# Attention step: the order of its products on TensorE, and the dealing of its output products over the column groups

## The chip, the cores and the metric

The kernel runs on one core of one Trainium2 chip. The metric is the device time of one execution in microseconds (us), the median over the runs of a kernel. A core has a matrix engine (TensorE, PE in the profile, with its weight loads shown apart as PEld), VectorE (DVE), ScalarE (ACT), GpSimd (POOL) and SyncE (SP), which issues most of the DMAs. Each engine works through a list of instructions of its own, in the order in which the program wrote them.

## The reference

Eight batches of eight heads go through attention over 576 positions with windows, and the result goes through a mixture of eight experts, of which each token uses two.

```python
# attention: batch 8, heads 8, seq 576, head_dim 64
scores = q @ k.T / 8
rel = pos[:, None] - pos[None, :]
mask_plain = (rel >= 0) & (rel < 32)                         # heads 0 to 3
mask_dil = (rel >= 0) & (rel < 128) & (rel % 4 == 0)         # heads 4 to 7
attn = softmax(where(mask, scores, -1e9))
x = (attn @ v) as rows of 512 per token                      # 4608 tokens
# experts: D 512, E 8, F 1024
noisy = x @ w_gate + log1p(exp(x @ w_noise)) * noise
top2 = the two largest of noisy; weights = softmax over the two
out[token] = sum over the two: weight * (relu(x @ w1[e]) @ w2[e])
```

## The kernel before

The program has an attention stage and an expert stage. The change lies in the attention stage.

**Attention.** The work is cut into 24 steps. Two batches make a unit `u` (four units), a unit has two groups `g` (first the four heads with the dilated mask, then the four with the plain one), and a group has three steps `st`; step `k` is `3 * g + st`. With the layout chosen, a query block of 32 rows sees 64 keys, so the products are small. One step does this:

- `qk(k)`: the mask is put into the PSUM tile `s` by two products with an identity (L360, 128 columns of weights, bf16), then 24 products of queries and keys add the scores (L371). Each of them has 32 columns of weights, and its 32 output partitions say which of the four column groups of TensorE it uses. VectorE then takes the maximum of each row (L376) and subtracts it, writing `a` (L377). There is one buffer of `s`.
- `expo(k)`: ScalarE takes the exponential of `a` into `pe` (L382).
- `ptr(k)`: six transposes of `pe` through TensorE into the PSUM tiles `pp` (L396, 128 columns), which ScalarE copies to `pt` in two copies (L397).
- `pv(k)`: 24 output products of `pt` and the values into `o` (L414, 32 columns of weights, 130 moving columns, the last of a head being the sum of the row). VectorE computes the reciprocal of the sums (`den`, L421 and L423) and the scaled `x` (L426).
- `move_x(k)` and `store_x(k)`: ScalarE moves a part of `x` (L434), and SP writes it to DRAM (L439, L441).
- `x_transpose(k)`: six transposes of `x` into `xtp` (L449, 128 columns) and two copies to `xt` on ScalarE (L451).
- `gate_mm(k)`: eight products of `xt` with the gate's weights (L471, 32 columns) and copies to `gs` on ScalarE (L476, L497).
- `gate_front(u, st)`: three transposes of `gs` (L509, 128 columns) and one VectorE reduction (L510), three times for each unit when the unit is done.

A matmul of f32 operands appears in the trace as two records where its weights have 32 columns, so 24 products are 48 records.

The steps are staggered in a loop over `i`: an iteration runs `qk(i)`, `move_x(i - 2)`, `ptr(i - 1)`, `store_x(i - 2)`, `x_transpose(i - 2)`, `expo(i)`, `pv(i - 1)`, `gate_front` if one is due and `gate_mm(i - 2)`, in this order. Nothing reorders what the program writes: the order of calls is the order on each engine. Between the calls, `micro(n)` takes the next few small operations from the generators `gate(t0, n)`, which choose the experts for blocks of tokens (VectorE operations of 0.1 to 0.6 us, L524 to L628), and `fillers(kb)` runs what `at(kb, ...)` put on a slot; an iteration has the slots `2 * i` and `2 * i + 1`. The loads of the next keys, queries and values and of the first expert's weights hang on such slots.

**Experts.** After the loop the eight experts run one after another (`up`, L826, and `down_tile`, L868), with the gathers of their tokens (L770, L778), weights and scatters (L845) planned by a clock of TensorE columns. The first expert's tokens are gathered and split (L792, L797, L798, through the same PSUM tag `tin` as `xtp`) while the attention still runs.

Of the kernel before, what the change touches and what calls it, by code (L numbers as in the profile page):

```python
# [46 lines left out]
def attention_moe_kernel(ctx, tc, qt, kp, kd, vpl, vdl, w_gate, w_noise, noise, w1, w2, out, CAPS=(1216, 1216, 1216, 1184, 1184, 1152, 1152, 1152), SPLITS=(0, 384, 896)):  # L47
# [306 lines left out]
    def qk(k):  # L354
        g, st = divmod(k, 3)
        ty = 1 - g % 2
        s = aps.tile([128, 8, 2, 64], F32, name="s", tag="s")
        for e in (0, 4):
            n = min(4, 6 - e)
            tensor.matmul(s[:, e:e + n], lhsT=identb,  # L360
                          rhs=masks[ty][:, 6 * st + e:6 * st + e + n].unsqueeze(2).to_broadcast([128, n, 2, 64]),
                          start=True, stop=False, skip_group_check=True)
        for e in range(6):
            for qd in range(4):
                if ty == 0:
                    x = qd // 2
                    b, ub = divmod(12 * st + 6 * (qd % 2) + e, 18)
                else:
                    x = qd
                    b, ub = divmod(6 * st + e, 9)  # L370
                tensor.matmul(s[32 * qd:32 * qd + 32, e], lhsT=QV[ty][:, b, x, 32 * ub:32 * ub + 32],  # L371
                              rhs=KV[ty][:, :, b, x, 32 * ub:32 * ub + 64],
                              start=False, stop=True, skip_group_check=True)
# [26 lines left out]
    def pv(k):  # L400
# [4 lines left out]
        for hh in range(4):  # L405
            for r, a, jp, b, ub in blocks(st, ty):
# [517 lines left out]
    fronts = {6 * u + 6 + st: (u, st) for u in range(U) for st in range(3)}  # L924
# [39 lines left out]
    for t0, n, kb in ((0, 9, 17), (9, 9, 29), (18, 6, 39), (24, 3, 41), (27, 6, 51)):  # L964
        at(kb, lambda t0=t0, n=n: gens.append(gate(t0, n)))
    L0 = 12 * (U - 1)
    at(29, lambda: (new_idx(0), gens.append(idx_late(list(gens), 0, SPLITS[1], lambda: x_block(0)))))
    at(41, lambda: gens.append(idx_late(list(gens), SPLITS[1], SPLITS[2], lambda: x_block(1))))
# [39 lines left out]
    for i in range(NS + 2):  # L1008
# [3 lines left out]
        early[0] = False  # L1012
        if i < NS:
            qk(i)
# [4 lines left out]
        if 1 <= i <= NS:  # L1019
            ptr(i - 1)  # L1020
        micro(2)
        micro(2)
        fillers(2 * i)
        if i >= 2:
            store_x(i - 2)
            x_transpose(i - 2)
        if i < NS:

            expo(i)
        micro(2)  # L1030
        if 1 <= i <= NS:
            pv(i - 1)
        micro(2)
        if i >= 2:
            if i in fronts:
                gate_front(*fronts.pop(i))
            gate_mm(i - 2)
# [4 lines left out]
    for f in fronts.values():  # L1042
# [191 lines left out]
```

## Time and profile before

| what | value |
|---|---|
| median of three runs | 1081.24 us (1080.13 to 1085.15) |
| span of the profiled execution | 1086.8 us; no time beside the span is given for it |
| PE busy | 1011.7 us (93%) |
| PEld busy | 855.7 us (79%) |
| DVE, ACT, POOL busy | 465.7, 319.4, 534.5 us |
| first mask product of the first step | 9.6 us |
| first product of the first expert | 227.24 us |

The attention stage is the first fifth of the span; from 227.24 us on TensorE works on the experts. The span of the profiled execution is 5.6 us above the median of the runs. A row of the timeline reads: start in us, length in us, engine, line, operation, tile written and tiles read, shape, count of records and, in brackets, how long the engine had been idle before and what ended it. "issue" is time in which an engine waited for nothing that the profile shows.

### The profile page before, as it was taken

The page shows a single profiled execution, that of the slowest core. Times are in us where ns is not written, and L with a number is a line of the kernel's source. Part 1 is how long each engine was busy: PE and PEld are TensorE (multiplying, and loading weights), DVE is VectorE, ACT ScalarE, POOL GpSimd, SP SyncE. Part 2 cuts the span into 40 slices and gives each one's busy share as a digit, 9 for nine tenths or more (in the row PEclk, how much of TensorE's full clock was granted, in tenths as well). Part 3 has the DMA queues.
Part 4 walks back from the last instruction along what each step waited for, and adds up shares of the span by engine and source line. Part 5 has one row for each costly group of instructions (what it writes and reads, how often), then busy time and mean ns, then how long its engine had stood idle before and what let it go on. Part 6 is the DMA issues. An engine that isn't in the chain of part 4 may idle for free. (4 is left out here: it accounts for less than half of the span.)

```text
span 1086.8 us, 18768 instructions
## 1 busy us (share of the span) xinstructions
PE 1011.7 (93%) x7274; PEld 855.7 (79%) x7275; DVE 465.7 (43%) x1060; ACT 319.4 (29%) x609; POOL 534.5 (49%) x727
## 2 busy tenths in 40 slices
PE   6896877778989999999999999999999999999996
PEld 4774655567878989988997889788978888888885
DVE  7673635635225444344434352435353434343221
ACT  6673534622113322222223131312131222222110
POOL 7004243455776655755644564466455645553112
PEclk9998887878999999999999999999999999999999
DMA  8898687455255243533533352426242623453123
GB/s 280 313 315 278 194 283 257 151 164 186 43 96 129 54 109 85 109 84 86 91 85 85 86 131 50 102 64 135 38 112 52 137 39 108 75 119 72 24 28 45
DMA packets 79214, 132.95 MB, mean 122 GB/s; under 512 B 31648, under 2 KB 41296, under 8 KB 77840
## 3 DMA queue, kind: packets, MB, share of 16 engines
q1 hardware_dynamic: 56768, 92.56, 27.6%
q0 software_dynamic: 22352, 39.15, 19.6%
q8 instruction: 58, 0.95, 0.4%
q14 instruction: 36, 0.29, 0.1%
HBM read 92.11 MB, written 39.54 MB: 121 GB/s over the span
## 5 line engine op out<-in xcount | busy, mean ns | idle before, releaser
L826 PE MATMUL up<-x,w1h 128*128 128x512 f32 (+4 forms) x1536 | 396.7, 344 | 10.9 <-issue 8.2
L778 POOL DMA_INDIRECT g<-xs,ixi x258 | 269.7, 1045 | 84.0 <-issue 78.6
L826 PEld LDWEIGHTS up<-x,w1h 128*128 128x128 f32 x1536 | 273.1, 189 | 37.2 <-issue 8.7
L826 PE MATMUL up<-x,w1l 128*128 128x384 f32 (+4 forms) x768 | 263.4, 343 | 0.0
L868 PE MATMUL dn<-w2h,hh 128*128 128x512 f32 x576 | 225.5, 392 | 0.0
L868 PE MATMUL dn<-w2l,hh 128*128 128x512 f32 x576 | 224.7, 390 | 0.0
L868 PE MATMUL dn<-w2h,hl 128*128 128x512 f32 x576 | 224.6, 390 | 0.0
L832 DVE SCALAR_TENSOR_TENSOR hl<-up,hh 128x384 fp32r<-128x384 f32 (+2 forms) x192 | 106.7, 557 | 249.1 <-ACT hh L830 187.0
L830 ACT ACTIVATE hh<-up 128x384 fp32r<-128x384 f32 (+4 forms) x192 | 94.6, 498 | 298.7 <-PE up L826 248.7
L845 POOL DMA_INDIRECT out_rows<-y,ixs x67 | 107.3, 1602 | 141.4 <-DVE y L877 119.0
L826 PEld LDWEIGHTS up<-x,w1l 128*128 128x128 f32 x768 | 145.4, 189 | 11.8
L877 DVE TENSOR_SCALAR y<-dn,ixs 128x512 f32<-128x512 f32 x63 | 47.3, 751 | 188.2 <-PE dn L868 163.5
L868 PEld LDWEIGHTS dn<-w2h,hl 128*128 128x128 f32 x576 | 108.4, 188 | 22.7
L868 PEld LDWEIGHTS dn<-w2h,hh 128*128 128x128 f32 x576 | 108.5, 188 | 22.0
L868 PEld LDWEIGHTS dn<-w2l,hh 128*128 128x128 f32 x576 | 108.5, 188 | 21.8
L797 ACT CAST x<-xr 128x512 fp32r<-128x512 f32 x67 | 40.5, 605 | 216.0 <-DVE xr L795 175.8
L306 POOL COPY spacer<-hh 1x1 f32<-1x1 f32 x72 | 26.4, 366 | 131.9 <-ACT hh L830 131.6
L628 POOL DMA_INDIRECT tab<-en,si x72 | 71.8, 998 | 36.1 <-issue 16.2
L798 DVE TENSOR_TENSOR x<-xr,x 128x512 fp32r<-128x512 f32 x67 | 44.7, 667 | 17.9 <-ACT x L797 12.4
L371 PE MATMUL s<-kt,qt 128*32 128x128 f32 x1152 | 41.2, 288 | 9.9 <-DMA qt<-in_qt 5.4
L371 PEld LDWEIGHTS s<-kt,qt 128*32 128x32 f32 x1152 | 32.5, 115 | 20.3 <-issue 19.6
L708 DVE TENSOR_TENSOR w1l<-ws,w1h 128x1024 fp32r<-128x1024 f32 x32 | 38.8, 1218 | 20.8 <-ACT w1h L706 10.9
(186 smaller groups left out, 867.2 us busy)
## 6 DMA issues: line engine op xcount, KB each, us to landing
ws<-in_moe_w SPq DMA_DIRECT2D x36, 512.0 KB
ws<-in_moe_w SPq DMA_DIRECT2D x112, 128.0 KB
out_rows<-zero SPq DMA_DIRECT2D x38, 256.0 KB
vd<-in_vdl SPq DMA_DIRECT2D x24, 390.0 KB
vp<-in_vpl SPq DMA_DIRECT2D x16, 585.0 KB
qt<-in_qt SPq DMA_DIRECT2D x14, 576.0 KB
xs<-x SPq DMA_DIRECT2D x24, 256.0 KB
kt<-in_kd SPq DMA_DIRECT2D x16, 320.0 KB
```

The costliest lines, as they stand in the source:

```text
L371: tensor.matmul(s[32 * qd:32 * qd + 32, e], lhsT=QV[ty][:, b, x, 32 * ub:32 * ub + 32], rhs=KV[ty][:, :, b, x, 32 * ub:32 * ub + 64], star ...
L628: ins = gpsimd.indirect_dma_start(out=tab, out_offset=bass.IndirectOffsetOnAxis(ap=si[:, kq, t:t + 1], axis=0), in_=en[:, kq, t], in_offse ...
L708: return lambda: vector.tensor_tensor(b, s, a.bitcast(F32), op=OP.subtract)
L778: gpsimd.indirect_dma_start(out=g[:, j], out_offset=None, in_=xq, in_offset=bass.IndirectOffsetOnAxis(ap=IX[e][1][:, r0 // 32 + j:r0 // 32 ...
L797: scalar.copy(xh[:, :, o:o + rn], xr[:, :, 0:rn])
L798: return lambda: vector.tensor_tensor(xl[:, :, o:o + rn], xr[:, :, 0:rn], xh[:, :, o:o + rn].bitcast(F32), op=OP.subtract)
L826: tensor.matmul(p[:, 0:n], lhsT=a[:, 128 * f:128 * f + 128], rhs=b[:, kc, 0:n], start=(i == 0), stop=(i == 11))
L830: scalar.activation(hh[:, f, 0:n], p[:, 0:n], AF.Relu)
L832: vector.scalar_tensor_tensor(hl[:, f, 0:m], p[:, 0:m], 0.0, hh[:, f, 0:m].bitcast(F32), op0=OP.max, op1=OP.subtract)
L845: ins = gpsimd.indirect_dma_start(out=out, out_offset=bass.IndirectOffsetOnAxis(ap=sc[0:rn, t, 1:2], axis=0), in_=y[0:rn], in_offset=None, ...
L868: tensor.matmul(p[0:rn], lhsT=a[:, f, o:o + rn], rhs=b[:, f % 2], start=(i == 0), stop=(i == 23))
L877: vector.tensor_scalar(y[0:rn], p[0:rn], wsc, None, op0=OP.mult)
```

## The change

The mask products get a function of their own, `mask_scores(k)`, and the loop is written in another order: first what uses 128 columns of weights (`x_transpose`, `gate_front`, the mask, `ptr`), then what uses 32 (`qk`, `gate_mm`, `pv`). `x_transpose` and `gate_mm` now belong to step `i - 3`, one iteration later than before; the last three are caught up at the end. `gate_front` is one iteration later as well, and the slots on which the generators start are moved by one. `expo(i)` is written behind `pv(i - 1)`. In `pv`, the 16 products of rows 0 to 3 come first, in turn over the four column groups, and then the 8 of rows 4 and 5, for the heads in the order 0, 2, 1, 3.

```diff
+    def mask_scores(k):
+        s = SC[k] = aps.tile([128, 8, 2, 64], F32, name="s", tag="s")
+        for e in (0, 4):
+            n = min(4, 6 - e)
+            tensor.matmul(s[:, e:e + n], lhsT=identb,
...
     def qk(k):
-        s = aps.tile([128, 8, 2, 64], F32, name="s", tag="s")
-        for e in (0, 4):
-            n = min(4, 6 - e)
-            tensor.matmul(s[:, e:e + n], lhsT=identb,
...
+        s = SC.pop(k)
...
     def pv(k):
-        for hh in range(4):
-            for r, a, jp, b, ub in blocks(st, ty):
+        bl = list(blocks(st, ty))
+        for hh, rows in [(hh, bl[0:4]) for hh in range(4)] + [(hh, bl[4:6]) for hh in (0, 2, 1, 3)]:
+            for r, a, jp, b, ub in rows:
                 qd, c0 = (r, hh) if r < 4 else (2 * (r - 4) + hh // 2, 4 + hh % 2)
...
-    fronts = {6 * u + 6 + st: (u, st) for u in range(U) for st in range(3)}
+    fronts = {6 * u + 7 + st: [(u, st)] for u in range(U - 1) for st in range(3)}
+    fronts[6 * U + 1] = [(U - 1, 0), (U - 1, 1)]
+    fronts[6 * U + 2] = [(U - 1, 2)]
...
-    for t0, n, kb in ((0, 9, 17), (9, 9, 29), (18, 6, 39), (24, 3, 41), (27, 6, 51)):
+    for t0, n, kb in ((0, 9, 18), (9, 9, 30), (18, 6, 40), (24, 3, 42), (27, 6, 50)):
         at(kb, lambda t0=t0, n=n: gens.append(gate(t0, n)))
...
     for i in range(NS + 2):
         micro(2)
+        if 3 <= i < NS:
+            x_transpose(i - 3)
+        micro(2)
+        for f in fronts.pop(i, []):
+            gate_front(*f)
         if i < NS:
-            qk(i)
+            mask_scores(i)
+        micro(2)
+        if 1 <= i <= NS:
+            ptr(i - 1)
         micro(2)
         if i >= 2:
             move_x(i - 2)
         micro(2)
-        if 1 <= i <= NS:
-            ptr(i - 1)
-        micro(2)
-        micro(2)
         fillers(2 * i)
         if i >= 2:
             store_x(i - 2)
-            x_transpose(i - 2)
         if i < NS:
-            expo(i)
+            qk(i)
         micro(2)
+        if 3 <= i < NS:
+            gate_mm(i - 3)
         if 1 <= i <= NS:
             pv(i - 1)
-        micro(2)
-        if i >= 2:
-            if i in fronts:
-                gate_front(*fronts.pop(i))
-            gate_mm(i - 2)
+        if i < NS:
+            expo(i)
+        for k in {NS: (NS - 3, NS - 2), NS + 1: (NS - 1,)}.get(i, ()):
+            micro(2)
+            x_transpose(k)
+            gate_mm(k)
         micro(2)
         micro(2)
         fillers(2 * i + 1)
```

**TensorE, one step with a `gate_front`.** Lines in the changed program stand seven or eight further down: L362 is the mask, L378 `qk`, L403 `ptr`, L422 `pv`, L457 `x_transpose`, L479 `gate_mm`, L517 `gate_front`. Before:

```order
L360 MATMUL s<-mask_144,identb 128x512
L360 LDWEIGHTS identb
L360 MATMUL s<-mask_144,identb 128x256
L371 MATMUL s<-kt_98,qt_100 32x128 x24
L396 MATMUL pp_194<-ident,pe 128x128 x4
L396 MATMUL pp_195<-ident,pe 128x128 x2
L449 MATMUL xtp<-ident,x 128x128 x6
L414 MATMUL o<-vd,pt 32x130 x24
L509 MATMUL gt<-ident,gs 128x128 x3
L471 MATMUL pp_195<-xt,wg 32x128 x4
L471 MATMUL pp_195<-xt,wg 32x64 x4
```

The same engine in the changed program, from one `x_transpose` to the next:

```order
L457 MATMUL xtp<-ident,x 128x128 x6
L517 MATMUL gt<-ident,gs 128x128 x3
L362 LDWEIGHTS identb
L362 MATMUL s<-mask_144,identb 128x512
L362 LDWEIGHTS identb
L362 MATMUL s<-mask_144,identb 128x256
L403 MATMUL pp_194<-ident,pe 128x128 x4
L403 MATMUL pp_195<-ident,pe 128x128 x2
L378 MATMUL s<-kt_98,qt_100 32x128 x24
L479 MATMUL pp_195<-xt,wg 32x128 x4
L479 MATMUL pp_195<-xt,wg 32x64 x4
L422 MATMUL o<-vd,pt 32x130 x24
```

The change between 128 and 32 columns of weights came six times in such a step (four times without `gate_front`) and now comes twice; the transposes of `pe` (`ptr`) stood behind the next step's `qk` and now stand ahead of it.

**ScalarE, the same step.** Before, from the move of `x` to the copies of `gs`:

```order
L434 COPY x<-x 32x2x128 x2
L397 COPY pt<-pp_194 128x512
L397 COPY pt<-pp_195 128x256
L451 COPY xt<-xtp 128x384 x2
L382 ACTIVATE pe<-a 128x6x2x64
L476 COPY gs<-pp_195 64x6x32 x2
```

In the changed program:

```order
L459 COPY xt<-xtp 128x384 x2
L404 COPY pt<-pp_194 128x512
L404 COPY pt<-pp_195 128x256
L442 COPY x<-x 32x2x128 x2
L484 COPY gs<-pp_195 64x6x32 x2
L389 ACTIVATE pe<-a 128x6x2x64
```

The exponential moved from ahead of the copies of `gs` to behind them, and the copies of `xt` to the front.

**VectorE, the step in which the second `gate` runs**: the last rows ahead of the maximum of the next step's scores. Before:

```order
L549 MAX u_1897<-nl 128x8 x6
L423 RECIPROCAL den<-den 128x12
L553 MAX_INDEX c_1899<-u_1897,nl 128x8 x6
L426 TENSOR_TENSOR x<-o,den 128x384 x2
L553 MAX_INDEX c_1899<-u_1897,nl 128x8 x3
L557 TENSOR_TENSOR wd<-u_1897 128x9
L560 CAST xf<-c_1899 128x18
L564 TENSOR_TENSOR oh<-i_168,xf 128x72 x2
L567 TENSOR_TENSOR ob<-oh 128x72
L572 TENSOR_SCALAR ns<-xf 128x9
L574 TENSOR_SCALAR ns<-ns 128x2x9
L376 TENSOR_REDUCE mx<-s 128x12
```

In the changed program (L383 is the maximum, L434 the scaled `x`):

```order
L541 TENSOR_TENSOR c_1930<-c_1930,nl 128x72
L434 TENSOR_TENSOR x<-o,den 128x384 x2
L548 TENSOR_TENSOR l_1929<-l_1929,c_1930 128x72
L550 TENSOR_TENSOR l_1929<-l_1929,nz 128x72
L552 TENSOR_TENSOR nl<-l_1929,lg 128x72
L557 MAX u_1928<-nl 128x8 x9
L561 MAX_INDEX c_1930<-u_1928,nl 128x8 x9
L565 TENSOR_TENSOR wd<-u_1928 128x9
L568 CAST xf<-c_1930 128x18
L572 TENSOR_TENSOR oh<-i_168,xf 128x72 x2
L575 TENSOR_TENSOR ob<-oh 128x72
L383 TENSOR_REDUCE mx<-s 128x12
```

The operations of `gate` that stood between `den` and `x` now stand behind `x`, in one piece ahead of the next maximum.

More of the change, by code (lines that the diff above doesn't have):

```diff
@@ L352, in attention_moe_kernel @@
     SB, PE_, PT, XG, XT, GS = {}, {}, {}, {}, {}, {}
-    def qk(k):
+    SC = {}
+    def mask_scores(k):
         g, st = divmod(k, 3)
         ty = 1 - g % 2
-        s = aps.tile([128, 8, 2, 64], F32, name="s", tag="s")
+        s = SC[k] = aps.tile([128, 8, 2, 64], F32, name="s", tag="s")
         for e in (0, 4):
@@ L362, in qk @@
                           start=True, stop=False, skip_group_check=True)
+    def qk(k):
+        g, st = divmod(k, 3)
+        ty = 1 - g % 2
+        s = SC.pop(k)
         for e in range(6):
@@ L962, in x_block @@
             plan(US_X[bi - 1] + 3.0 * i, lambda t=t: split_first(bi, t))
-    for t0, n, kb in ((0, 9, 17), (9, 9, 29), (18, 6, 39), (24, 3, 41), (27, 6, 51)):
+    for t0, n, kb in ((0, 9, 18), (9, 9, 30), (18, 6, 40), (24, 3, 42), (27, 6, 50)):
         at(kb, lambda t0=t0, n=n: gens.append(gate(t0, n)))
     L0 = 12 * (U - 1)
-    at(29, lambda: (new_idx(0), gens.append(idx_late(list(gens), 0, SPLITS[1], lambda: x_block(0)))))
-    at(41, lambda: gens.append(idx_late(list(gens), SPLITS[1], SPLITS[2], lambda: x_block(1))))
+    at(30, lambda: (new_idx(0), gens.append(idx_late(list(gens), 0, SPLITS[1], lambda: x_block(0)))))
+    at(42, lambda: gens.append(idx_late(list(gens), SPLITS[1], SPLITS[2], lambda: x_block(1))))
     at(2, setup_a)
@@ L1025, in attention_moe_kernel @@
             store_x(i - 2)
-            x_transpose(i - 2)
+        if i < NS:
[3 more added lines that the diff above has]
+            gate_mm(i - 3)
+        if 1 <= i <= NS:
+            pv(i - 1)
         if i < NS:
             expo(i)
-        micro(2)
-        if 1 <= i <= NS:
-            pv(i - 1)
-        micro(2)
-        if i >= 2:
-            if i in fronts:
-                gate_front(*fronts.pop(i))
-            gate_mm(i - 2)
+        for k in {NS: (NS - 3, NS - 2), NS + 1: (NS - 1,)}.get(i, ()):
+            micro(2)
+            x_transpose(k)
+            gate_mm(k)
         micro(2)
@@ L1041, in attention_moe_kernel @@
     early[0] = True
-    for f in fronts.values():
+    for f in sum(fronts.values(), []):
         gate_front(*f)
```

## The prediction

> **What bounds the kernel now.** I read the page first, then the busy time by stage, the waits of the attention stage, and last the timeline of single steps, because an average over the stage hides which wait ends last. Here and below, 0.5% of the time, 5.4 us, is about what a measurement of this kernel can tell from no change.
>
> ```profile
> span 1086.8 us, 18768 instructions
> ...
> PE 1011.7 (93%) x7274; PEld 855.7 (79%) x7275; DVE 465.7 (43%) x1060; ACT 319.4 (29%) x609; POOL 534.5 (49%) x727
> ...
> PEclk9998887878999999999999999999999999999999
> ```
> ```profile
> 40.00:60.00 20.00, 20.00 (x462) 16.48 (x460) 12.85 (x31) 14.77 (x36) 0.43 (x1) 1.00 0.92 320
> 80.00:100.00 20.00, 13.59 (x189) 10.49 (x189) 7.32 (x25) 6.74 (x14) 8.77 (x16) 0.80 0.95 318
> 140.00:160.00 20.00, 15.09 (x213) 9.98 (x206) 6.11 (x21) 5.95 (x14) 11.53 (x22) 0.75 0.88 285
> 340.00:1087.00 747.00, 734.66 (x3660) 634.76 (x3658) 291.17 (x458) 174.59 (x291) 386.00 (x470) 1.00 0.40 84
> ```
>
> The columns behind the length of a stretch are PE, PEld, DVE, ACT and POOL, the granted clock, the DMAs' share and GB/s. From 340 us on PE is busy 735 of 747 us at full clock: the experts are bound by PE, so what the attention stage saves or loses arrives at the end. From 40 to 60 us PE is busy all the time. From 80 to 100 and from 140 to 160 it is not, the clock is 0.80 and 0.75, and the DMAs are at 0.95 and 0.88. So the attention stage is of two kinds. How much of each, the mask's rows tell (48 records in 24 steps):
>
> ```profile
> L360 PE MATMUL s<-mask,identb x48: 270/378/609, 9.6 to 197.8; 128*128 128x512 bf16 x24, 128*128 128x256 bf16 x24
> ```
> ```profile
> PEld s L371 <- issue: 19.6, 28, 4.4
> PE o L414 <- ACT pt L397: 11.9, 7, 4.3
> DVE mx L376 <- remote: 20.6, 3, 8.4
> ```
>
> Between the first and the last step lie 188 us for 23 steps, 8.2 us each. Nine of these 23 gaps are 5.37 to 6.01 us (five of them with a `gate_front`); the other 14 hold about 60 us more than that, in which engines wait for nothing that the profile shows ("issue") or for "remote", DVE once for 8.4 us.
>
> An undisturbed step without `gate_front`, and behind it the end of the next step, which has one:
>
> ```profile
> 41.90 0.50 PE L360 MATMUL s<-mask,identb 128*128 128x512 bf16 x2
> 42.33 1.52 PE L371 MATMUL s<-kt,qt 128*32 128x128 f32 x48
> 43.78 0.87 PE L396 MATMUL pp<-ident,pe 128*128 128x128 f32 x6
> 44.49 0.82 PE L449 MATMUL xtp<-ident,x 128*128 128x128 f32 x6
> 45.24 1.56 PE L414 MATMUL o<-vp,pt 128*32 128x130 f32 x44
> ...
> 47.28 0.50 PE L360 MATMUL s<-mask,identb 128*128 128x512 bf16 x2
> ...
> 50.63 1.78 PE L414 MATMUL o<-vp,pt 128*32 128x130 f32 x48
> 52.35 0.55 PE L509 MATMUL gt<-ident,gs 128*128 128x128 f32 x3
> 52.82 0.54 PE L471 MATMUL pp<-xt,wg 128*32 128x128 f32 x16
> 53.29 0.50 PE L360 MATMUL s<-mask,identb 128*128 128x512 bf16 x2
> ```
>
> From mask to mask these take 5.38 and 6.01 us, PE in one row without a wait.
>
> **The change, PE's work.** A `gate_front` adds 0.63 us. Its three transposes cost 3 x 0.118 (six take 0.71, from 43.78 to 44.49), so the two extra changes between 128 and 32 columns cost 0.27, 0.14 each. The change goes from four to two of them without `gate_front`, from six to two with it: 0.27 and 0.54 us saved. The dealing: 48 records of `qk`, in turn over the groups, take 1.45 us for 128 columns, so 130 columns in turn should take 1.47; the old order takes 1.72 (50.63 to 52.35): 0.25 saved. PE's work of a step becomes 4.86 and 5.22 us.
>
> [...]
>
> **The change, the loop that it closes.** Before, `ptr` of a step stood behind the next step's `qk` and had more than 2 us to spare. Now `ptr(i - 1)` stands ahead of `qk(i)`, and it needs the exponential of step i - 1, which needs the subtraction, the maximum and `qk(i - 1)`. So one step cannot be shorter than that chain. Its pieces:
>
> ```profile
> 39.62 0.38 ACT L397 COPY pt<-pp 128x256 f32<-128x256 f32 x1
> 108.52 0.96 DVE L377 TENSOR_TENSOR a<-s,mx 128x768 f32<-128x768 f32 x1
> 109.51 0.90 ACT L382 ACTIVATE pe<-a 128x768 f32<-128x768 f32 x1 [0.31 <-DVE a L377]
> 111.35 1.52 PE L371 MATMUL s<-kt,qt 128*32 128x128 f32 x48
> 112.94 0.96 DVE L376 TENSOR_REDUCE mx<-s 128x12 f32<-128x768 f32 x1 [1.03 <-PE s L371]
> 114.00 0.96 DVE L377 TENSOR_TENSOR a<-s,mx 128x768 f32<-128x768 f32 x1
> 124.08 0.86 ACT L397 COPY pt<-pp 128x512 f32<-128x512 f32 x2 [4.49 <-remote]
> 124.72 2.83 PE L414 MATMUL o<-vd,pt 128*32 128x130 f32 x44 [4.26 <-ACT pt L397]
> ```
>
> From the start of `qk` to the maximum 1.59, to the subtraction 1.06, to the exponential 0.99 (108.52 to 109.51), the exponential 0.90. From ScalarE to PE: the first copy of the pair ends 0.86 - 0.38 = 0.48 behind 124.08, at 124.56, and PE starts at 124.72: 0.16. Then six transposes and the change to 32 columns, 0.75 (as from 44.49 to 45.24). Sum 5.45. To that comes the first weight load, which can't be made ahead any more; no row has it alone, it lies between nothing and 0.15 (about the 0.14 of a change of columns). I take 5.5, with 5.45 and 5.6 as the ends. PE's own work, 4.86 or 5.22, fits under it, so PE now waits 0.3 to 0.6 us a step. The mask doesn't add to this: it needs the subtraction, about 2.1 us behind `qk`, and PE comes to it only after `gate_mm`, `pv` and `x_transpose`. ScalarE doesn't either: the copies of `gs` (five small ones, about 1.1 us), which now stand ahead of the exponential, follow a `gate_mm` that ends 0.5 us behind `qk`, so they are done 1.6 us behind it, and the subtraction at 2.1.
>
> [...]
>
> **The sum.**
> 1. The nine undisturbed gaps: four without `gate_front` +0.12 each, five with it -0.51 each: -2.1 us. With the loop at 5.45 it is -2.5, at 5.6 -1.2.
> 2. The disturbed ones. PE's clock falls after a long wait, and then PE's work is what counts: `pv` took 2.83 for 44 records at 124.72 and 1.56 at 45.24, 1.8 times. A step wholly at that clock has 9.7 us of PE work before and 8.75 after, against a loop of about 7.3 (1.8 us more in `qk` and `ptr`): -0.95, with `gate_front` -1.4. I count seven such stretches, each about three quarters of a step: -5. Bounds: 0 (the wait sets the end, not the work behind it) and -9 (14 x 0.52 to 0.79, at full clock).
> 3. VectorE in steps with `gate`. The loop leaves 5.5 - 2.0 = 3.5 us between a subtraction and the next maximum, and nothing to spare. Before, a late maximum was free for about 1.3 us (the mask came 3.5 us behind `qk`, the subtraction ends at 2.2).
>
> ```profile
> 68.39 0.96 DVE L377 TENSOR_TENSOR a<-s,mx 128x768 f32<-128x768 f32 x1
> 72.48 0.71 DVE L549 MAX8 u<-nl 128x8 f32<-128x8 f32 x9
> 74.39 0.97 DVE L376 TENSOR_REDUCE mx<-s 128x12 f32<-128x768 f32 x1
> ```
> ```profile
> L708 DVE TENSOR_TENSOR w1l<-ws,w1h 128x1024 fp32r<-128x1024 f32 x32 | 38.8, 1218 | 20.8 <-ACT w1h L706 10.9
> ```
>
> A gate's piece took 5.1 us between subtraction and maximum (69.3 to 74.4). The changed program has such a piece whole in the second and the last gates of the stage and a w1 split of 1.2 us in two steps: four steps some 1.5 to 2 us too long, one 0.4, less about 2.4 that such steps cost before: +4. Bounds 0 (hidden in waits that are there anyway) and +7.
> 4. The end: `x_transpose` and `gate_mm` of one more step come behind the last `pv`, 0.75 + 0.47 us, partly beside the wait for the last `x`: +1, 0 to +2. At the start three steps do without them, but there PE waits for the first loads.
> 5. DMAs: the same ones in the same order on SP and POOL, moved by half a step at most, and the 60 us of waits for instructions and data I take as they are: 0. A single wait there is 4 to 8 us, so one more or one fewer is the bound: -8 to +8.
>
> Sum -2.1 - 5 + 4 + 1 = -2.1. The profiled span, 1086.8, would become 1084.7. No run's own time is given beside it and it lies 5.6 above the median, so I take the difference off the median: 1081.2 - 2.1, about **1079 us**; its own range, for this case alone, is 1076 to 1085.
>
> **Rivals.**
> *PE's saving arrives (1070).* In the 14 disturbed steps PE is late, the loop isn't what ends last, and each gains PE's full saving, ten or eleven times 0.52 and four times 0.79, -8.9; with -2.1 of the nine and the VectorE and end terms hidden in waits, -11. For it: 20 us of PE's waits stand ahead of `qk` alone, and work after them runs at a lower clock. Against it: a step that waits for instructions is no shorter for having less to do. Were there no loop at all, all 24 steps would give 15 x 0.52 + 9 x 0.79 = 15 us, 1066.
> *VectorE and the loop (1088, slower).* The place is the maximum of the scores in the steps with `gate` and the w1 splits; the price is the upper bound of term 3, +7, and it decides once the work between a subtraction and the next maximum is over 3.5 us in more than four steps. With the loop at 5.6 (-1.2), no gain in the disturbed steps and +1 to +2 at the end: 1081.2 + 7 = 1088. For it: PE's order has no slack left, so a wait of DVE or ACT (20.6 us for "remote") also falls on every step. Against it: several of these steps stand beside waits of 8 us and more.
> *The dealing does nothing.* Inside the loop's step, PE's 0.25 us is slack, so this part alone would be invisible; that is within the forecast.
>
> **How the numbers follow.** The forecast, little change, has 0.45; the faster rival 0.31; the slower one 0.24. About 0.07 of the forecast's chance lies beyond 5.4 us on the fast side and 0.02 on the slow side: faster 0.38, same 0.36, slower 0.26. The range takes both rivals in, with a little beyond for term 5: 1067 to 1090.
>
> **What would show it.** In the trace after: mask to mask near 5.5 us with and without `gate_front`; PE idle 0.3 to 0.6 us ahead of `ptr`, released by the exponential; `pv` near 1.47 us; the maximum late in the steps with a gate. I am wrong if `ptr` doesn't wait and steps run in 4.9 us, if the waits for instructions come at other places and in other lengths, or if the first product of the experts moves by more than 5 us from 227.2.

## The result, and the profile after

The changed kernel takes 1089.70 us (median of seven runs, 1084.63 to 1093.69) against 1081.24 us before (seven runs beside it, 1076.35 to 1085.15): 1.0075 times the time, with a 95% interval of 1.0046 to 1.0103, so 8 us slower. Little change, 1079 us, was forecast.

The profiled execution after, its page and two of the stretches that were shown of before (columns: PE, PEld, DVE, ACT, POOL, granted clock, share of the DMAs, GB/s):

```profile
span 1086.4 us, 18747 instructions
...
PE 1008.1 (93%) x7274; PEld 849.9 (78%) x7275; DVE 466.3 (43%) x1060; ACT 320.8 (30%) x609; POOL 531.4 (49%) x727
...
PEclk9998888798989999999999999999999999999998
```
```profile
40.00:60.00 20.00, 17.73 (x415) 14.63 (x403) 13.09 (x31) 14.43 (x35) 0.42 (x1) 1.00 0.94 307
340.00:1087.00 747.00, 736.14 (x3668) 636.23 (x3666) 293.41 (x461) 175.49 (x292) 383.62 (x471) 1.00 0.40 84
```

PE's busy time from 40 to 60 us fell from 20.00 to 17.73, but so did the number of its records, from 462 to 415: PE now waits there. What the order and the dealing save shows in single steps. A step with `gate_front`, before and after:

```profile
53.29:59.30 6.01, 6.01 (x136) 4.82 (x130) 3.67 (x9) 4.00 (x9) 0.43 (x1) 1.00 0.80 264
60.50:67.05 6.55, 5.45 (x131) 4.71 (x129) 3.67 (x8) 4.05 (x9) 0.00 (x0) 1.00 1.00 331
```

PE is busy for 5.45 us where it was busy for 6.01, and the step takes 6.55 us, not 6.01. The stage ends about where it did: the first product of the experts moved from 227.24 to 225.71 us. The spans of the two profiled executions (1086.8 and 1086.4) don't show the difference of the medians; the second set below says where they differ.

Two steps of after without `gate_front`, on PE:

```profile
41.35 0.49 PE L362 MATMUL s<-mask,identb 128*128 128x512 bf16 x2
42.15 0.87 PE L403 MATMUL pp<-ident,pe 128*128 128x128 f32 x6 [0.31 <-ACT pe L389]
42.95 1.52 PE L378 MATMUL s<-kt,qt 128*32 128x128 f32 x48
...
47.09 0.49 PE L362 MATMUL s<-mask,identb 128*128 128x512 bf16 x2
```

From mask to mask 5.74 us (5.39 in the step before it), and PE waits 0.31 us for the exponential ahead of `ptr`: the loop that the forecast drew. The loop rests on `qk` staying behind a waiting `ptr`, and here it does: `ptr` starts at 42.15, `qk` at 42.95. The last section has rows of other products that start out of the program's order.

Steps with `gate_front`, PE and then ScalarE:

```profile
56.69 1.52 PE L422 MATMUL o<-vd,pt 128*32 128x130 f32 x48
58.14 0.88 PE L457 MATMUL xtp<-ident,x 128*128 128x128 f32 x6
60.12 0.55 PE L517 MATMUL gt<-ident,gs 128*128 128x128 f32 x3 [1.10 <-ACT xt L459]
60.50 0.49 PE L362 MATMUL s<-mask,identb 128*128 128x512 bf16 x2
60.83 0.82 PE L403 MATMUL pp<-ident,pe 128*128 128x128 f32 x6
...
66.67 0.55 PE L517 MATMUL gt<-ident,gs 128*128 128x128 f32 x3 [1.10 <-ACT xt L459]
67.05 0.38 PE L362 MATMUL s<-mask,identb 128*128 128x512 bf16 x1
```
```profile
58.66 0.90 ACT L389 ACTIVATE pe<-a 128x768 f32<-128x768 f32 x1 [1.09 <-DVE a L384]
59.59 0.86 ACT L459 COPY xt<-xtp 128x384 f32<-128x384 f32 x2
```

These take 6.55 us (60.50 to 67.05), not 5.5, and `ptr` no longer waits. The tag `tin` has two PSUM buffers. `x_transpose` takes both, `gt` comes right behind and needs the first one back, so it waits for the copy of `xt`, and on ScalarE that copy stands behind the exponential.

### The profile page after: what moved, and what is told of

It is laid out like the page before. It is cut to its first block, busy times and chain, and to the rows that moved or that the text cites. A ratio compares the mean times of both kernels' runs of the same rounds, so it can differ in the third digit from the quotient of the medians.

```text
span 1086.4 us, 18747 instructions
## 1 busy us (share of the span) xinstructions
PE 1008.1 (93%) x7274; PEld 849.9 (78%) x7275; DVE 466.3 (43%) x1060; ACT 320.8 (30%) x609; POOL 531.4 (49%) x727
## 5 line engine op out<-in xcount | busy, mean ns | idle before, releaser
L786 POOL DMA_INDIRECT g<-xs,ixi x258 | 264.8, 1026 | 84.9 <-issue 79.8
L383 DVE TENSOR_REDUCE mx<-s 128x12 f32<-128x768 f32 x24 | 22.9, 956 | 70.9 <-remote 40.6
L806 DVE TENSOR_TENSOR x<-xr,x 128x512 fp32r<-128x512 f32 x67 | 44.7, 667 | 17.9 <-ACT x L805 13.7
L306 POOL COPY spacer<-x 1x1 f32<-1x1 f32 x13 | 3.2, 246 | 91.8 <-DVE x L434 91.7
L378 PE MATMUL s<-kt,qt 128*32 128x128 f32 x1152 | 42.5, 283 | 5.8 <-issue 5.0
```

The costliest lines, as they stand in the source:

```text
L306: gpsimd.tensor_copy(spacer, late["x"])
L786: gpsimd.indirect_dma_start(out=g[:, j], out_offset=None, in_=xq, in_offset=bass.IndirectOffsetOnAxis(ap=IX[e][1][:, r0 // 32 + j:r0 // 32 ...
L806: return lambda: vector.tensor_tensor(xl[:, :, o:o + rn], xr[:, :, 0:rn], xh[:, :, o:o + rn].bitcast(F32), op=OP.subtract)
```

## The experiments

They ran in three sets, each on a chip of its own, beside runs of the kernel before: 1028.74 us on the first set's chip, 1083.4 on the second's, 1029.68 on the third's. Ratios are to the kernel before on the same chip, traces are compared within chips of one speed. There is no profile of the kernel before on the two faster chips; deal_only, whose time is that of before, stands for it. A trace is one execution, and its time lies up to 3.6 us off the median of its kernel (after_p 1087.85 against 1091.46), so sums of traces and ratios differ by some us. "up" is the first product of the first expert, "tab" the last write of GpSimd's table of token rows, both in us; the rest of the span behind "up" is the last column.

| kernel, set | ratio [95%] | up | tab behind up | span behind up |
|---|---|---|---|---|
| deal_only, 1 | 1.0003 [0.9984, 1.0022] | 189.8 | 64.0 | 839.8 |
| order_only, 1 | 1.0098 [1.0067, 1.0130] | 188.5 | 70.4 | 846.1 |
| front_first, 1 | 1.0113 [1.0084, 1.0142] | 189.4 | 70.5 | 848.0 |
| ptr_behind, 1 | 1.0161 [1.0125, 1.0197] | 200.6 | 69.0 | 845.2 |
| before_p, 2 | the kernel before | 225.8 | 70.2 | 856.6 |
| late_gates, 2 | 1.0026 [1.0005, 1.0046] | 225.8 | 74.6 | 857.9 |
| after_p, 2 | 1.0072 [1.0044, 1.0100] | 226.4 | 76.5 | 859.7 |
| micro9, 2 | 1.0097 [1.0068, 1.0126] | 238.5 | 70.2 | 855.2 |
| fronts_back, 3 | 1.0055 [1.0032, 1.0079] | 190.4 | 65.8 | 841.5 |
| micro9_end, 3 | 1.0085 [1.0059, 1.0112] | 190.9 | 68.9 | 843.9 |
| late_gates_2, 3 | 1.0077 [1.0050, 1.0103] | 189.1 | 72.6 | 849.5 |
| after_p2, 3 | 1.0100 [1.0076, 1.0124] | 190.6 | 69.7 | 845.3 |

### First set: which part, and is it the wait of gt

**front_first**: the changed kernel with `gate_front` ahead of `x_transpose`.

```diff
+        for f in fronts.pop(i, []):
+            gate_front(*f)
         if 3 <= i < NS:
             x_transpose(i - 3)
         micro(2)
-        for f in fronts.pop(i, []):
-            gate_front(*f)
```

> The changed kernel with one edit: gate_front ahead of x_transpose instead of behind it. Theory A (PSUM buffers): in a step with gate_front the tile gt takes a buffer of the tag tin that x_transpose has just filled, so its transposes wait 1.1 us for ScalarE's copy of xt, which stands behind the exponential; that lengthens nine steps from 5.5 to 6.55 us. With gate_front first its buffer is long free: those steps come to 5.5 us, 9 x 1.05 = 9.4 us less than the changed kernel, about 1080. Theory B (the rival on record: the loop and late maxima on VectorE in the steps with a gate): nothing of that is touched, 1089 as the changed kernel, steps with gate_front stay at 6.5. Theory C (waits for instructions fell elsewhere): no change beyond the spread, 1085 to 1092, whatever the steps show.

Measured 1.0113. `gt` no longer waits, but the step is as long (6.55 us, not 5.5): now the second `xtp` is the third tile of the tag, and it waits the same 1.1 us for the same copy. The edit moved the wait, so it says nothing on what the wait is worth.

**deal_only**: the kernel before with the new `pv`.

```diff
-        for hh in range(4):
-            for r, a, jp, b, ub in blocks(st, ty):
+        bl = list(blocks(st, ty))
+        for hh, rows in [(hh, bl[0:4]) for hh in range(4)] + [(hh, bl[4:6]) for hh in (0, 2, 1, 3)]:
+            for r, a, jp, b, ub in rows:
```

> The kernel before with the new dealing of the output products alone. If PE's work sets the undisturbed steps there, pv goes from 1.72 to 1.47 us and a step from 5.38 to 5.13 and from 6.01 to 5.76: 24 x 0.25 = 6 us less, 1075. If the waits for data and instructions set the stage's length (C), the steps get shorter and the waits longer, and the time stays within 2 us of 1081.

Measured 1.0003: nothing. Steps on PE do get shorter, by what the forecast took for the dealing (5.14 us without `gate_front`, 5.75 with it, against 5.38 and 6.01 with the old dealing, on this kind of chip too, in late_gates_2), and the time doesn't. Near the end of the stage PE waits for the gathered tokens of the first expert, four times, 5.4 us together. A PE that is early would only wait longer there; without a profile of before on this chip that is likely and not shown.

**order_only**: the changed kernel with the old loop in `pv`.

> The changed kernel with the old dealing of the output products. A and B both say that PE has 0.3 to 1.1 us to spare in a step of the changed order, so that 0.25 us more of pv costs nothing: 1089 as the changed kernel, within 2 us, with pv at 1.72 and steps at 5.4 to 5.6 and 6.55. If PE's work were the limit, 24 x 0.25 = 6 us more, 1095.

Measured 1.0098, as much as the whole change on such a chip (1.0100), with steps of the length that was expected (5.40 and 5.43 us, 6.56 with `gate_front`): the loss is in the order, not in the dealing. And the table says where, as far as the traces show it: `up` is no later than in deal_only, 6.3 us lie behind it.

**ptr_behind**: the changed kernel with `ptr(i - 1)` moved behind `qk(i)` and `gate_mm`.

```diff
-        if 1 <= i <= NS:
-            ptr(i - 1)
-        micro(2)
...
         if 3 <= i < NS:
             gate_mm(i - 3)
+        if 1 <= i <= NS:
+            ptr(i - 1)
+        micro(2)
         if 1 <= i <= NS:
             pv(i - 1)
```

> The changed kernel with ptr of the step before put behind qk and gate_mm, so that its exponential has time again: four changes of columns a step instead of two, no loop from step to step; gate_front still behind x_transpose. A: the loop is worth little by itself (5.13 instead of 5.5 us in 15 steps, -5.5), gt still waits about 0.5 us for the copy of xt, so its nine steps come to 6.0 (-5): about 1078. B: late maxima cost nothing any more, and this alone takes all of the loss away and the saved changes and the dealing remain: 1074. C: 1085 to 1092.

Measured 1.0161, slower than any of the three theories had it. Here the steps themselves got longer (6.2 to 6.7 us); `pv` stands directly behind the transposes whose copies it needs, but the waits that the trace names in such a step are short (0.17 to 0.30 us each), so the reason is not shown. `up` is 11 us later. A loss inside the loop does show in `up` when it is large enough; that of the change doesn't.

### Second set: the routing chain

What lies between `up` and the loss is the second expert. Which tokens it gets is known when the gates are through: GpSimd writes a row of the table for each token, SP loads the expert's row numbers from that table, GpSimd gathers the tokens, VectorE and ScalarE split them (`xr` and `x`). The change moves that chain without touching its code. Its small operations are run by calls of `micro(2)` between the calls of the loop; there are nine of them in an iteration before, and eight after (both can be counted in the loop). The second gate starts on slot 30, not 29. Together this puts the end of that gate, and the load of the first row numbers that waits for it, one iteration later. SP's order, before:

```
L441 DMA xs<-x 64x1x256 x2
L743 DMA ixf<-tab 128x3x4
L125 DMA vp_95<-in_vpl 64x2340 x2
L988 DMA out_rows<-zero 128x512 x3
L439 DMA xs<-x 256x1x256
L441 DMA xs<-x 64x1x256 x2
```

and after:

```
L449 DMA xs<-x 64x1x256 x2
L125 DMA vp_95<-in_vpl 64x2340 x2
L999 DMA out_rows<-zero 128x512 x3
L447 DMA xs<-x 256x1x256
L449 DMA xs<-x 64x1x256 x2
L751 DMA ixf<-tab 128x3x4
```

The load has moved behind eight more DMAs, the next step's stores among them (57 stores stand ahead of it before, 60 after), and GpSimd makes four writes to the table fewer (40, not 44) ahead of its second block of gathers. In the two traces of the forecast the load starts at 171.43 us before and at 181.59 after. This is theory D. Theory A is the waits for `tin`, theory C the loads and the "waits for instructions", as the expectations call the idle time that the profile puts down to "issue" or "remote"; what it is, no trace says.

**micro9**: the changed kernel with a ninth call.

```diff
             gate_mm(i - 3)
+        micro(2)
         if 1 <= i <= NS:
             pv(i - 1)
```

> The changed kernel with one call micro(2) added ahead of pv, so that an iteration takes nine such calls, as before the change, and not eight. Nothing of TensorE's order changes. In the program's order the load of the first expert's row numbers (ixf) then stands behind 57 store DMAs again, not 60, and GpSimd writes four tab rows more ahead of the second block of gathers. Theory D (the generators that choose the experts fall behind by one iteration, GpSimd ends its tab writes 5 to 6 us later, and the second expert waits for its gathered tokens): last tab write 4 to 6 us earlier against the first up product than in the changed kernel, the 3.4 us wait of up near 75 us after that product gone, ratio to the kernel before 0.997 to 1.003 (about 8 us below the changed kernel). Theory A (the waits of the transposes for a buffer of tag tin): steps with gate_front still 6.5 us, ratio as the changed kernel's, 1.007 to 1.011. Theory C (the end of the stage is set by loads): the ratio stays above 1.005.

Measured 1.0097, so the time did not come back, against theory D; A and C had such a ratio. The two halves of the trace disagree, though. Behind `up` the expectation holds: the last table write is again 70.2 us behind it, as in before_p, and the rest of the span is 855.2 us, 4.5 less than in after_p. But `up` itself came 12.2 us later than in after_p. That part lies in waits with no releaser: PE has 35.2 us of "issue" ahead of `up`, against 23.6 in after_p (and 12.7 in before_p). One such stretch, PE, VectorE and ScalarE, and the stretch by engine:

```profile
158.91 0.31 PE L479 MATMUL pp<-xt,wg 128*32 128x64 f32 x1 [0.45 <-issue]
...
161.05 0.38 PE L422 MATMUL o<-vp,pt 128*32 128x130 f32 x1 [0.29 <-issue]
161.75 2.83 PE L422 MATMUL o<-vp,pt 128*32 128x130 f32 x44 [0.33 <-issue]
...
161.87 0.96 DVE L383 TENSOR_REDUCE mx<-s 128x12 f32<-128x768 f32 x1 [10.38 <-remote]
...
162.02 0.64 ACT L484 COPY gs<-pp 64x192 f32<-64x192 f32 x2 [9.67 <-remote]
```
```profile
152.00:162.00 10.00, 3.92 (x28) 1.53 (x30) 0.14 (x1) 0.35 (x1) 6.89 (x13) 0.70 0.69 195
```

For 10 us PE advances by one to three records at a time, 0.7 or 1.4 us apart, and VectorE and ScalarE do next to nothing. Why the added call makes this worse on that chip stays open.

**late_gates**: the kernel before with the second gate and the first load of row numbers on slot 31, and nothing else of the change.

```diff
-    for t0, n, kb in ((0, 9, 17), (9, 9, 29), (18, 6, 39), (24, 3, 41), (27, 6, 51)):
+    for t0, n, kb in ((0, 9, 17), (9, 9, 31), (18, 6, 39), (24, 3, 41), (27, 6, 51)):
...
-    at(29, lambda: (new_idx(0), gens.append(idx_late(list(gens), 0, SPLITS[1], lambda: x_block(0)))))
+    at(31, lambda: (new_idx(0), gens.append(idx_late(list(gens), 0, SPLITS[1], lambda: x_block(0)))))
```

> The kernel before, with one thing of the change alone: the second gate and the load of the first row numbers start on slot 31, not 29. TensorE's, VectorE's and ScalarE's order of the attention products stays as before. In the program's order the first ixf load moves behind 60 store DMAs, and GpSimd has four tab rows fewer ahead of the second block of gathers. Theory D: first up product within 1 us of before, last tab write 4 to 6 us later, up waits 3 to 4 us near 75 us after its first product, ratio 1.006 to 1.010. Theory A or C (the order of the loop): ratio 0.998 to 1.002.

Measured 1.0026 [1.0005, 1.0046]: slower, by 2.7 us, a third of the loss. The value lies between the two expectations, and the interval reaches into that of A and C, not into that of D. `up` stayed (225.84 against 225.81) and the last table write came 4.4 us later, both as D expects; the single wait of `up` of 3 to 4 us did not come.

**after_p** and **before_p**: the changed kernel and the kernel before, for a pair of profiles on one chip.

> The changed kernel itself, unchanged, on the chip of the experiments. Theory D: ratio 1.007 to 1.011, first up product within 1.5 us of the kernel before, and the loss behind it: a wait of up of 3 to 5 us after a late load of ixt, with the granted clock at 0.5 to 0.75 for some 6 us behind that wait. Theory A: the first up product itself 5 us or more later than before.

> The kernel before itself, for a profile on the chip of the experiments. Theory D: last tab write 63 to 65 us after the first up product (64.0 in the kernel with the new dealing alone), no wait of up over 1 us in the first 150 us of the experts, granted clock 1.00 there. Theory C: first up product 2 us or more away from 189 us.

Measured 1.0072 for after_p. The numbers expected for before_p had been taken on the faster chip and don't hold here (70.2 us, not 63 to 65, from `up` to the last write). The writes of the table, of before_p and of after_p (the line gives shortest, median and longest in ns, then the first and the last start):

```profile
L628 POOL DMA_INDIRECT tab<-en,si x72: 955/962/1838, 85.3 to 296.0; - x72
```
```profile
L636 POOL DMA_INDIRECT tab<-en,si x72: 954/959/1692, 93.8 to 302.9; - x72
```

`up` moved by 0.55 us, the last write by 6.9, the rest of the span by 3.1. The wait of `up` of 3 to 5 us after a late load, which D expected, is not there. after_p has one wait of 6.0 us, for a gate's cast on VectorE, but it stands 18 us behind `up`, and from 226 to 260 us before_p is held up as much (PE busy 28.46 of 34 us, against 27.98). The two part later. PE from 300 to 320 us, of before_p and of after_p, and after_p's rows there:

```profile
300.00:320.00 20.00, 19.74 (x93) 16.55 (x93) 5.73 (x10) 2.82 (x6) 14.94 (x22) 0.92 0.71 125
300.00:320.00 20.00, 15.30 (x52) 10.77 (x52) 3.72 (x6) 1.94 (x4) 13.88 (x24) 0.74 0.55 96
```
```profile
305.04 0.38 SPq L755 DMA_DIRECT2D ixt<-tab  x1
305.67 0.59 PE L876 MATMUL dn<-w2h,hh 128*128 128x512 f32 x1 [0.60 <-issue]
307.74 0.23 SPq L760 DMA_DIRECT2D ixs<-tab  x1
307.77 0.58 PE L876 MATMUL dn<-w2l,hh 128*128 128x512 f32 x1 [1.51 <-issue]
307.82 0.60 ACT L838 ACTIVATE hh<-up 128x512 fp32r<-128x512 f32 x1 [9.98 <-remote]
310.18 1.03 POOL L786 DMA_INDIRECT g<-xs,ixi  x1 [0.16 <-POOL spacer L306]
```

While GpSimd makes its last writes to the table, PE gets through one product in 0.7 to 2.1 us, and it goes on (307.77) as the last of SP's loads of the second expert's row numbers starts (307.74), ahead of the gathers (310.18); in before_p these are 300.39, 300.35 and 302.73. Counted by products, the same sixty of `up` and `dn`, from about 67 us behind `up` on, take 19.4 us in before_p, 21.4 in micro9, 22.9 in late_gates and 24.8 in after_p, and 20.0 and 24.2 in the two traces of the forecast, before and after. In the main the stretch is longer where the table is later. (On the faster chips it takes 15.2 in all eight traces.) So on this kind of chip the loss that the traces show lies behind `up` as well, 5.4 us of it in this stretch. What PE waits for there is named "issue" and stays open; it is not the second expert's tokens. Near 940 us before_p loses 3.0 us that after_p does not, at this wait, and the spans differ by only 3.7 us:

```profile
937.59 0.50 PE L826 MATMUL up<-x,w1h 128*128 128x256 f32 x2 [1.89 <-DVE hl L832]
```

The forecast's trace of before has such a wait there too, and that of after doesn't. Of the 8.1 us between the medians the rest is not shown.

### Third set: the same on a chip with few such waits

**late_gates_2**: the same kernel as late_gates.

> The same kernel as late_gates, for the chip that this call falls on. On the chip of the first four experiments, where TensorE hardly waits for instructions, theory D expects the last tab write 4 to 6 us later, a wait of up of 3 to 4 us near 75 us after its first product, span minus first up product 844 to 848 us (839.8 with the new dealing alone), ratio 1.005 to 1.009. On the other chip: ratio 1.001 to 1.005, as measured. Theory A: 0.998 to 1.002 on either.

Measured 1.0077 [1.0050, 1.0103], 8.4 us, where the whole change costs 9.2 on this chip. PE's order is the old one here; one gate and one load start two slots later, and that is enough for a loss of this size. It is not the change's share of it, though: the last table write comes 72.6 us behind `up` here and 69.7 in the changed kernel. The chain in its trace, by time, engine after engine:

```profile
261.65 0.98 POOL L628 DMA_INDIRECT tab<-en,si  x1 [0.16 <-issue]
...
263.79 0.38 SPq L747 DMA_DIRECT2D ixt<-tab  x1
...
269.33 1.08 POOL L757 TENSOR_SCALAR ixi<-ixt 32x38 int32<-32x38 int32 x4 [4.80 <-DMA ixt<-tab]
...
270.82 1.04 POOL L778 DMA_INDIRECT g<-xs,ixi  x1 [0.16 <-POOL spacer L306]
...
277.32 0.71 DVE L795 STREAM_TRANSPOSE xr<-g 128x512 f32<-128x512 f32 x1 [5.95 <-DMA g<-xs,ixi]
...
278.06 0.62 ACT L797 CAST x<-xr 128x512 fp32r<-128x512 f32 x1 [8.71 <-DVE xr L795]
278.59 1.09 ACT L830 ACTIVATE hh<-up 128x320 fp32r<-128x320 f32 x3
...
279.75 0.87 PE L826 MATMUL up<-x,w1h 128*128 128x320 f32 x2 [5.65 <-ACT hh L830]
```

And where the table is done in time, in deal_only:

```profile
253.78 0.98 POOL L629 DMA_INDIRECT tab<-en,si  x1 [0.16 <-issue]
...
255.91 0.38 SPq L748 DMA_DIRECT2D ixt<-tab  x1
...
261.00 1.04 POOL L779 DMA_INDIRECT g<-xs,ixi  x1 [0.16 <-POOL spacer L306]
...
270.03 0.70 DVE L796 STREAM_TRANSPOSE xr<-g 128x512 f32<-128x512 f32 x1
...
270.77 0.62 ACT L798 CAST x<-xr 128x512 fp32r<-128x512 f32 x1 [1.24 <-DVE xr L796]
```

PE does not wait for the second expert's tokens as such. It is still at the first expert's products when the late tokens hold up VectorE, VectorE holds up the cast on ScalarE, and behind that cast stand the activations `hh` of the first expert (ScalarE's part of them; `hl` is VectorE's), three at once when it is over; without them the PSUM buffers of `up` don't come free. In deal_only the transpose waits for nothing. The 5.65 us of the wait are not all. The same trace by stretches of 3 us, PE's busy time first, the granted clock third from the end:

```profile
275.00:278.00 3.00, 0.00 (x0) 0.00 (x0) 0.68 (x1) 0.00 (x0) 2.51 (x5) 0.92 0.17 44
278.00:281.00 3.00, 1.25 (x5) 1.28 (x6) 1.98 (x8) 1.61 (x4) 2.39 (x3) 0.50 0.82 122
281.00:284.00 3.00, 3.00 (x13) 3.00 (x13) 0.33 (x3) 0.44 (x1) 2.46 (x5) 0.50 0.17 53
284.00:287.00 3.00, 3.00 (x21) 3.00 (x20) 1.96 (x6) 0.96 (x2) 2.44 (x4) 0.94 0.68 83
```

PE works again from 279.75, but at 0.50 of its clock until 284.40, 4.6 us (single records of 320 columns take 0.47 us there and 0.31 from 284.40 on): 13 records in three microseconds in which deal_only does 22 or 23. That is some 2 us more, and part of why the rest of the span grows by more than the wait: the forty products in which the wait falls take 13.7 us here and 5.9 in deal_only. PE is idle from 274.1 us; the clock is 1.00 from 272 to 275 and 0.92 in the mean from 275 to 278. If it went from 1.00 to 0.50 at once, the 0.92 puts that at about 277.5, an estimate.

**after_p2**: the changed kernel on this chip.

> The changed kernel itself beside the other three. On the chip of the first four experiments: ratio 1.008 to 1.012, first up product 187 to 191 us, span minus first up product 845 to 848 us. On the other chip: ratio 1.005 to 1.010, first up product 225 to 228 us, span minus first up product 859 to 861 us.

Measured 1.0100; `up` at 190.6 and 845.3 us of span behind it, all as expected; the last table write is 69.7 us behind `up`. Its longest wait of `up` is 3.4 us, for `hh`, as in order_only and front_first, and the forty products around it take 11.0 us (11.5 in those two), against 5.9 in deal_only. That is 5.1 us of the 6.3 by which the spans of after_p2 and deal_only differ.

**fronts_back**: the changed kernel with `gate_front` behind `pv`, one iteration earlier, and the slots of before.

```diff
+    fronts = {6 * u + 6 + st: [(u, st)] for u in range(U) for st in range(3)}
...
+    for t0, n, kb in ((0, 9, 17), (9, 9, 29), (18, 6, 39), (24, 3, 41), (27, 6, 51)):
...
-        for f in fronts.pop(i, []):
-            gate_front(*f)
         if i < NS:
             mask_scores(i)
...
         micro(2)
+        for f in fronts.pop(i, []):
+            gate_front(*f)
         micro(2)
         fillers(2 * i + 1)
```

(The loads of row numbers are on 29 and 41 again.)

> The changed kernel with gate_front at the end of its iteration, behind pv, one iteration earlier, and with the generators and the row-number loads on the slots of before (17, 29, 39, 41, 51 and 29, 41). The program's order on GpSimd and SyncE is then that of the kernel before (57 store DMAs ahead of the first ixf load, four tab rows more ahead of the second block of gathers); TensorE keeps the changed order except for gt. Theory D (the routing chain is one iteration late): last tab write 70 to 72 us after the first up product (76.5 in the changed kernel on one chip), span minus first up product 3 to 5 us less than the changed kernel's, ratio to before 0.996 to 1.003. Theory A (waits for tin buffers): gt no longer waits for xt at the head of a step, steps with gate_front 5.4 to 5.8 us, and the first up product 3 us or more earlier. Theory C (loads and waits for instructions set the end of the stage): first up product within 2 us of the kernel before, or later as in the kernel with the ninth call, whatever the steps take.

Measured 1.0055: half of the loss is back (4.7 us below after_p2). The last table write is 65.8 us behind `up`, 3.9 less than after_p2, and the span behind `up` is 3.8 less. It came earlier than was expected for D, since that number was taken on the slower chip; the ratio stayed above D's 1.003. The wait for `hh` is gone, and the forty products take 5.9 us as in deal_only; of what is left, 4.5 us, the trace shows 2.3: 1.6 some 10 us behind `up`, where `up` waits for VectorE's `hl`, and 0.6 in `up` itself. The steps with `gate_front` take 6.6 to 7.3 us here, as the second half of `x_transpose` now waits, 1.1 us for the copy of `xt` and 1.4 for VectorE's `lg`: like front_first this moved theory A's wait and didn't take it away. What that wait is worth stays untested. At `up` no price of it is seen: on the faster chips the kernels that have it, with `ptr` ahead of `qk`, reach `up` at 188.5 to 190.9 us, and deal_only at 189.8.

**micro9_end**: the ninth call at the end of the iteration.

> As the kernel with the ninth call micro(2), but with the call at the end of the iteration and not ahead of pv. Theory D alone: last tab write 70 us after the first up product, span minus first up product 4 us below the changed kernel's. Theory C (where waits for instructions fall depends on which instructions stand where, so the place of the call decides): the first up product comes back from 238.5 to 226 to 230 us on that chip, ratio 0.998 to 1.005. If instead the ninth call's own VectorE work costs the 12 us: first up product again 236 to 240 us, ratio 1.008 to 1.011.

Measured 1.0085, `up` at 190.9, where after_p2 has it: at this place and on this chip the ninth call costs the stage nothing. Place and chip both differ from micro9's, so what cost 12 us there isn't settled. Nor does the call bring much: the first gathers start 3.4 us earlier (161.96 against 165.39), but the last table write is only 0.9 us nearer to `up` and the rest of the span 1.4 us shorter. GpSimd waits for the second load of row numbers in between, and its first gather behind that comes at 195.5, 3.1 us later than in after_p2. The call alone restores the order of the first load, not the time of the chain's end. The first transpose of the late tokens, in after_p2 and in micro9_end:

```profile
274.82 0.71 DVE L803 STREAM_TRANSPOSE xr<-g 128x512 f32<-128x512 f32 x1 [5.08 <-DMA g<-xs,ixi]
274.75 0.71 DVE L803 STREAM_TRANSPOSE xr<-g 128x512 f32<-128x512 f32 x1 [1.92 <-DMA g<-xs,ixi]
```

The tokens come at the same time in both. PE hardly waits for `hh` in micro9_end (the forty products take 6.3 us) since it gets there 3.1 us later, held up by shorter waits ahead of it.

So what counts is the time from the last table write to PE's arrival at those forty products. It is 16.6 to 16.8 us in deal_only, fronts_back and ptr_behind, where they take 5.9 us; 13.6 in micro9_end, where they take 6.3; and 8.8 to 10.9 in the other four, where they take 11.0 to 13.7, late_gates_2 most. By these eight the order of PE's products makes no difference to it. In deal_only the chain has thus some 3 us to spare, and a delay costs time only when these are used up. It isn't all: ptr_behind, fronts_back and micro9_end are slower than before with little or nothing of this wait.

## Why the prediction was wrong

- **The step that failed is term 5**: "the same ones in the same order on SP and POOL, moved by half a step at most", priced at 0. The order is not the same. The first row-number load moved by a whole step, past eight DMAs, from 171.43 to 181.59 us, and GpSimd's last table write with it, from 72.6 to 77.4 us behind `up`. The program's order showed this before any run; the working compared the rows on PE, ScalarE and VectorE, not those on SP and GpSimd. What it costs: on the faster chips a delay of that gate and that load alone loses 8.4 us (late_gates_2), with the table 2.9 us later than in the changed kernel, and in the changed kernel's own trace the wait behind it is worth 5.1 us. On a chip like the one of the forecast the delay alone loses 2.7 of 8.1 us (late_gates), and the traces of the changed kernel show some 4 and 5 us in the stretch where the table ends, in waits of another kind. The term's bound of +8 covers the loss by luck: it stood for one wait more or fewer inside the stage.
- **Where the loss would arrive** was wrong with it. The prediction read the experts as bound by PE from 340 us on and took the attention stage's end for the place where everything is paid. The stretch from 227 to 340 us, in which the second expert's tokens are routed, was not read.
- **Term 1** (-2.1): the loop is there, 5.39 and 5.74 us where 5.5 was forecast, with `ptr` waiting 0.28 and 0.31. A first weight load, 0 to 0.15 us in the forecast's sum, has no time of its own in the rows: in the trace of after it starts together with `ptr`, at 42.15, 0.05 us behind the end of the exponential (42.10). In the steps with `gate_front` the size was off: 6.55, not 5.5. Their wait for a `tin` buffer behind the exponential was overlooked, though the tag was in the text. So five gaps cost 0.54 more each instead of 0.51 less, and eight steps from the fifth mask to the thirteenth take 48.5 us in after_p against 46.4 in before_p: +2.1. The count was off too: not nine of the 23 gaps lie between 5.37 and 6.01 us but twelve (those of 5.46, 5.39 and 5.92 as well), and one is shorter, so ten were disturbed and not 14.
- **Terms 2 to 4** (-5, +4, +1) can't be told apart; together with term 1 they come to +0.55 in the pair (from 225.81 to 226.36) and to -1.5 in the two traces of the forecast. At the fifteenth mask the kernels of the pair stand at 109.3 and 109.9 us again, behind waits in both. The gain forecast for the disturbed steps did not arrive. PE's "issue" waits ahead of `up` grew instead, from 12.7 to 23.6 us in the pair and from 19.1 to 25.6 in the forecast's traces, which fits the lower bound of term 2, "the wait sets the end, not the work behind it".
- **The rivals.** PE's saving did not arrive. The dealing does nothing: shown (1.0003). The slower rival had the time, 1088, but not the mechanism: its place was the maximum of the scores, and `up` would have had to come later. That the measured 1089.70 lies in the range of 1067 to 1090 is therefore luck.
- **The signs.** Three that the text named came: steps without `gate_front` near 5.5 us, `ptr` waiting for the exponential, and, as a sign of being wrong, "issue" waits in other lengths. That `up` would move by more than 5 us was the wrong one to ask for: the loss came without it.

What stays open: on the slower chips, what PE waits for while the table ends and the part of the loss that no trace shows; why the ninth call made the "issue" waits longer there; on the faster ones, about half of the loss, which stays when the chain is early again (fronts_back). None of the kernels is faster than the one before.

## What to carry to other kernels

When a loop is written in another order, list what each queue does in the new order, also those that the change doesn't mean: here one call fewer per iteration and a start one slot later put a small DMA eight places back in SP's queue. Such a delay alone cost 2.7 us on one chip and 8.4 on another, and undoing it won back about half of the loss. Ask of each side chain (routing, index loads, gathers) when its last result is needed, and read that stage, even if it lies behind the one that is edited. A side chain can have slack (some 3 us in deal_only), and then only what goes beyond it costs time. A saving of PE's time need not arrive: in deal_only the steps shown are 0.24 and 0.26 us shorter and the ratio is 1.0003. That such steps end in a wait for data that comes at its own time is likely and not shown.

## What was not expected of the hardware

- A pause of PE cost more than its length: in late_gates_2, behind the 5.65 us wait, the granted clock was 0.50 for 4.6 us of work, some 2 us more. In after_p2, where the wait ends at 277.25 after 3.35 us, it was 0.78 from 276 to 279 and 0.65 from 279 to 282; in deal_only, without such a wait, 1.00 from 264 to 288. In the trace of before it was 0.50 from 124 to 128 us, behind the wait of 4.26 us that ends at 124.72 (the row that term 2 goes by).
- Chips differ: the same kernel takes 1028.74 and 1029.68 us on two of them and 1083.4 on a third. On the slower one PE crawls while VectorE and ScalarE stop for some 10 us ahead of `up` (10.38 and 9.67 in the rows of micro9). From 95 to 190 us VectorE is busy for 43.23 us in the trace of before and 45.37 in that of after, on the forecast's chip, and for 61.71 to 64.37 us in five traces of the faster ones (deal_only, order_only, late_gates_2, fronts_back, after_p2). The load of the DMAs doesn't explain it alone: their share is 0.69 in micro9's stretch, and 0.02 from 300 to 303 us in the trace of after, where PE has three records in 3 us.
- Products with 32 columns of weights did not all start in the order of the program. In after_p2 `gate_mm` (L479) stands wholly ahead of `pv` (L422), and yet:

```profile
71.55 0.27 PE L422 MATMUL o<-vd,pt 128*32 128x130 f32 x1
71.62 0.22 PE L479 MATMUL pp<-xt,wg 128*32 128x64 f32 x1
71.63 0.30 PE L422 MATMUL o<-vd,pt 128*32 128x130 f32 x1
71.63 0.22 PE L479 MATMUL pp<-xt,wg 128*32 128x64 f32 x1
```

The starts of the two alternate for about 0.1 us, by the trace's records; the trace of before has the like (its L471 starts at 46.59 us among rows of L414, which the program writes first). So "the order of calls is the order on each engine" doesn't hold to the last product. No run here tells whether the column groups are the reason.
